# Two MLPs over 512-token groups with the weights stationary in every matmul

## The chip, the cores and the metric

The kernel runs on one core of a Trainium2 chip. The metric is the device time of one execution in microseconds; less is better. Its engines are named here as the profile names them: PE (TensorE matmuls) with PEld (its weight loads), DVE (VectorE), ACT (ScalarE), POOL (GpSimd) and SP (SyncE, which issues the transfers).

## What is computed

A linear attention with a complex decay over 4 batches x 8 heads x 768 steps of width 48, whose output is 3072 tokens of 384 values; then an MLP with a squared ReLU (384 to 2048 to 384); then a gated MLP (384 to 1536 twice, back to 384) behind an RMS normalisation.

```python
def _moe_ref(x, w_in, w_out):
    h = x @ w_in
    r = np.maximum(h, 0.0)
    g = r * r
    return (g @ w_out).astype(np.float32)

def _moe2_ref(x, w_gate, w_val, w_out, rms_g):
    rms = np.sqrt(np.mean(x * x, axis=-1, keepdims=True) + 1e-06)
    xn = x / rms * rms_g
    g = xn @ w_gate
    silu = g * (1.0 / (1.0 + np.exp(-g)))
    val = xn @ w_val
    return (silu * val @ w_out).astype(np.float32)
...
    attn_out = _attn_ref(**attn_kwargs)
    x = attn_out.transpose(0, 2, 1, 3).reshape(B * S, H * D)
    x = _moe_ref(x=x, **moe_kwargs)
    return _moe2_ref(x=x, **moe2_kwargs)
```

## The kernel before

**Units.** The 3072 tokens are 24 units of 128. A unit `u` is one batch and one stretch of 128 steps; attention makes units in order, two (a pair) sharing the long element-wise chain on DVE and ACT (`norm`, seven `step`s, `tot`, `plevel`, `inv`). The per-unit part runs on PE with DVE and ACT between: `dtr` (tile dps), `score` (sps, then st on DVE), `yy` (yps), `state` (ups). From yps the output goes to `xt` (ACT), six small transfers on SP put its rows in place (`fix`), and `split_x` cuts it into a high and a low half, `xs[:, 0]` on ACT and `xs[:, 1]` on DVE. That DVE subtraction is the last step of a unit; from then on the first MLP can use it.

**Three passes.** Every product of the MLPs is three fp32r matmuls, high x high, high x low and low x high (`PASS`), so nine matmuls of 128 contraction rows make one 384-long product.

**First MLP.** It takes a group of two units (256 tokens, `GROUPS`) at a time. For each of 16 slices `f` of the hidden width, `mlp_h` runs nine matmuls with a weight block stationary and 256 tokens moving, into tile h of PSUM (3 buffers). ACT makes r, the square's high half (gs) and the full square back into h; DVE subtracts to get the low half (L821). `mlp_x` follows: six matmuls (two units x three passes) with the activations gs stationary and 384 columns of the second weight moving, so that x has tokens on the partitions. `store_x` writes x to DRAM (`xnd`, one token a row).

**Second MLP.** It takes three units (384 tokens, `G2`). `load_x` reads rows of `xnd`; `rms` squares and sums each row on ACT (`accum_out`) and scales it on DVE; `turn` transposes it on PE (three transposes for each of three column blocks, tile t) and ACT and DVE split it into ys. For each of 12 slices `mlp_g` and `mlp_v` run nine matmuls of 384 tokens with weights stationary, ACT takes the SiLU (tile t), DVE multiplies (uu), ACT and DVE split (us), and `mlp_o` runs nine matmuls with us stationary and 384 weight columns moving. `store` writes the rows of the output.

**What sets the order.** The program is in straight line. `Plan` holds jobs, each a generator of steps with an engine, a cost, buffers taken and given back, and needs; it simulates the engines and writes the instructions in the order that it finds, so each engine's queue is fixed when the program is built. A group's first `mlp_h` needs the xs of all its units (`need` in the loop over groups). Matmuls of the MLPs have a lower urgency than those of attention (`MLP_PE`). While attention runs, PE has both kinds of work; after it, MLP work alone. The weights arrive as words that are converted on ACT and DVE (`convert`); for the second MLP their tiles take the place of the first MLP's as the last group lets go of them.

Of the kernel before, what the change touches and what calls it, by code (L numbers as in the profile page):

```python
# [18 lines left out]
CH = 128  # L19
# [18 lines left out]
GROUPS = [[2 * i, 2 * i + 1] for i in range(12)]  # L38
# [11 lines left out]
def act(n):  # L50
    return 0.1 + 0.00083 * n
# [509 lines left out]
def general_path(tc, q, k, v, a_re, a_im, w, ident, gcol, out):  # L561
# [3 lines left out]
    with ExitStack() as ctx:  # L565
# [63 lines left out]
        with ExitStack() as c2:  # L629
# [33 lines left out]
            with tc.For_i(0, NT // 128, 1) as it:  # L663
# [22 lines left out]
                acc = ps.tile([128, DM], F32, tag="gacc", name="g_acc2")  # L686
                for f in range(F2):
# [5 lines left out]
                    nc.tensor.matmul(acc, lhsT=g, rhs=words(T_OUT2 + f // 2, f % 2), start=(f == 0), stop=(f == F2 - 1))  # L693
                o = sb.tile([128, DM], F32, tag="go", name="g_o")
                nc.vector.tensor_copy(o, acc)
                nc.sync.dma_start(out[bass.ds(it * 128, 128), :], o)
# [3 lines left out]
def kernel_body(ctx: ExitStack, tc, q, k, v, vt, a_re, a_im, w, rms_g, out):  # L700
# [8 lines left out]
    xnd = dram.tile([NT, DM], F32, name="xnd")  # L709
# [4 lines left out]
    psh = p1.enter_context(tc.tile_pool(name="psh", bufs=3, space=PSUM))  # L714
# [9 lines left out]
        sY=2, pe=4, xt=1, xs=2, h=3, xg=1, r=2, gs=3, x1=2, cr=2, cr2=4, xr=2, gv=3, ys=2, og=1, t=2, uu=2, us=3, ot=3,  # L724
# [60 lines left out]
    def fix(u, g, i):
        xt, sl = xt_t[g], slice(i * CH, (i + 1) * CH)
# [5 lines left out]
    def split_x(u, g, i):  # L792
        sl = slice(i * CH, (i + 1) * CH)
        xs = xs_t[g]
        yield from split(
            xs[:, 0, :, sl], xs[:, 1, :, sl], xt_t[g][:, 0:KT, sl], DM, rel=["xt"] if i else [], done=("xs", u)
        )

    def mlp_h(g, f):
        n = len(GROUPS[g]) * CH  # L800
        yield Op("pe", 1.06, acq=["h"], rel=["xs"] if f == F1 - 1 else [], done=("h", g, f), p=MLP_PE)
# [34 lines left out]

    def store_x(g, i, u):
        if i == 0:
            yield Op("dve", dve(DM), acq=["x1"], done=("xc", g, i))
            x = sb.tile([128, DM], F32, tag="x1", name="x1", bufs=2)  # L840
            nc.vector.tensor_copy(x, x_ps[g][i])
        else:
            yield Op("act", act(DM), acq=["x1"], done=("xc", g, i))
            x = sb.tile([128, DM], F32, tag="x1", name="x1", bufs=2)
            nc.scalar.copy(out=x, in_=x_ps[g][i])
# [282 lines left out]
```

## Time and profile before

| what | value |
|---|---|
| median of 3 runs | 1147.71 us (1145.86 to 1148.03) |
| span of the profiled execution | 1147.8 us |
| PE busy | 1084.5 us, 94% |
| PEld busy | 1039.6 us, 91% |
| DVE busy | 720.2 us, 63% |
| ACT busy | 628.3 us, 55% |
| POOL busy | 100.6 us, 9% |

The profiled execution's span lies within the three runs, 0.1 us from their median. The shares are averages over stages that differ: attention and the first MLP run together up to some 628 us, the end of the first MLP and the second MLP after it. So the rows below are read stage by stage: a table of busy time by stretches, the starts of matmuls in a timeline (the distance of two starts is what a group of matmuls takes; the durations in it overlap), and groups of instructions by shape.

### The profile page before, as it was taken

The page shows a single profiled execution, that of the slowest core. Times are in us where ns is not written, and L with a number is a line of the kernel's source. Part 1 is how long each engine was busy: PE and PEld are TensorE (multiplying, and loading weights), DVE is VectorE, ACT ScalarE, POOL GpSimd, SP SyncE. Part 2 cuts the span into 40 slices and gives each one's busy share as a digit, 9 for nine tenths or more (in the row PEclk, how much of TensorE's full clock was granted, in tenths as well). Part 3 has the DMA queues.
Part 4 walks back from the last instruction along what each step waited for, and adds up shares of the span by engine and source line. Part 5 has one row for each costly group of instructions (what it writes and reads, how often), then busy time and mean ns, then how long its engine had stood idle before and what let it go on. Part 6 is the DMA issues. An engine that isn't in the chain of part 4 may idle for free.

```text
span 1147.8 us, 20154 instructions
## 1 busy us (share of the span) xinstructions
PE 1084.5 (94%) x7876; PEld 1039.6 (91%) x7876; DVE 720.2 (63%) x1468; ACT 628.3 (55%) x1387; POOL 100.6 (9%) x90
## 2 busy tenths in 40 slices
PE   1679889999999999999999999999999999999997
PEld 0468679999999999999999988999999999999997
DVE  5999999998989988998622579632323232222221
ACT  3878866668577766665655899432323232222221
POOL 0011123022121221220000000000000000000000
PEclk9799999999999999999999999999999999999999
DMA  8733141423514423331001780010101000000000
GB/s 276 302 87 103 33 127 47 121 55 107 143 40 121 113 68 102 87 88 38 23 11 40 253 331 2 9 33 10 33 11 32 11 32 11 12 11 11 13 9 24
DMA packets 79063, 85.41 MB, mean 74 GB/s; under 512 B 47728, under 2 KB 74608, under 8 KB 78960
## 3 DMA queue, kind: packets, MB, share of 16 engines
q1 hardware_dynamic: 78824, 83.85, 23.8%
q8 instruction: 64, 1.05, 0.4%
q14 instruction: 39, 0.32, 0.1%
q10 hardware_dynamic: 136, 0.20, 0.1%
HBM read 64.23 MB, written 18.61 MB: 72 GB/s over the span
## 4 chain that ended last, share of the span: by engine, by line
PE 83%; DVE 6%; ACT 5%; DMA 3%; issue 1%; SPq 1%; DVEq 0%; ACTq 0%
PE h L807 17%; PE x L832 17%; PE v L992 12%; PE o L1028 12%; PE g L992 12%; PE sps L467 3%; PE dps L454 3%; DMA ws<-in_w 3%; PE yps L484 2%; PE ups L502 2%; PE yps L488 2%; ACT ws L535 1%; DVE ws L537 1%; DVE cr L541 1%; ACT cr L533 1%
## 5 line engine op out<-in xcount | busy, mean ns | idle before, releaser
L807 PE MATMUL h<-xs,w 128*128 128x256 f32 x1728 | 242.2, 285 | 3.0 <-ACT w L761 1.8
L832 PE MATMUL x<-w,gs 128*128 128x384 f32 x1152 | 241.3, 344 | 2.3 <-ACT gs L817 1.3
L807 PEld LDWEIGHTS h<-xs,w 128*128 128x128 f32 x1728 | 224.8, 189 | 7.0 <-ACT w L761 2.4
L832 PEld LDWEIGHTS x<-w,gs 128*128 128x128 f32 x1152 | 194.1, 190 | 6.8 <-DVE gs L821 2.2
L1014 DVE TENSOR_TENSOR uu<-t,v 128x384 f32<-128x384 f32 x96 | 53.1, 554 | 195.8 <-PE v L992 194.5
L1028 PE MATMUL o<-w,us 128*128 128x384 f32 x864 | 166.9, 336 | 2.9 <-ACT us L729 2.5
L992 PE MATMUL g<-ys,w 128*128 128x384 f32 x864 | 167.0, 337 | 1.3 <-DVE w L731 0.5
L992 PE MATMUL v<-ys,w 128*128 128x384 f32 x864 | 167.4, 338 | 0.0
L1028 PEld LDWEIGHTS o<-w,us 128*128 128x128 f32 x864 | 151.0, 188 | 5.1 <-ACT us L729 3.1
L992 PEld LDWEIGHTS g<-ys,w 128*128 128x128 f32 x864 | 151.7, 188 | 2.7 <-DVE w L731 1.4
L992 PEld LDWEIGHTS v<-ys,w 128*128 128x128 f32 x864 | 150.3, 188 | 0.1
L814 ACT ACTIVATE r<-h 128x256 f32<-128x256 f32 x192 | 72.9, 380 | 122.9 <-PE h L807 122.4
L1005 ACT ACTIVATE t<-g 128x384 f32<-128x384 f32 x96 | 47.3, 493 | 159.9 <-PE g L992 159.8
L729 ACT CAST us<-uu 128x384 fp32r<-128x384 f32 x96 | 49.2, 513 | 131.2 <-DVE uu L1014 131.2
L821 DVE TENSOR_TENSOR gs<-h,gs 128x256 fp32r<-128x256 f32 x192 | 80.4, 419 | 58.8 <-ACT h L819 57.9
L731 DVE TENSOR_TENSOR us<-uu,us 128x384 fp32r<-128x384 f32 x96 | 53.6, 558 | 50.2 <-ACT us L729 50.2
L817 ACT ACTIVATE gs<-r 128x256 fp32r<-128x256 f32 x192 | 80.3, 418 | 8.7 <-PE x L832 2.7
L512 POOL TENSOR_TENSOR Y<-W,pe 48x384 f32<-48x384 f32 x40 | 52.1, 1302 | 320.3 <-DVE W L508 174.6
L819 ACT ACTIVATE h<-r 128x256 f32<-128x256 f32 x192 | 71.2, 371 | 0.0
L467 PE MATMUL sps<-dq,dk 112*128 112x128 f32 x384 | 52.6, 282 | 4.3 <-ACT dq L456 1.8
L467 PEld LDWEIGHTS sps<-dq,dk 112*128 112x128 f32 x384 | 49.3, 197 | 6.2 <-ACT dq L456 2.7
L300 DVE TENSOR_TENSOR XY<-A 128x384 f32<-128x384 f32 x84 | 49.0, 583 | 2.2
(123 smaller groups left out, 1338.7 us busy)
## 6 DMA issues: line engine op xcount, KB each, us to landing
ws<-in_w SPq DMA_DIRECT2D x34, 768.0 KB
kb<-KP SPq DMA_DIRECT2D x20, 448.0 KB
kt<-kb SPq DMA_DIRECT2D x20, 448.0 KB
raw<-in_a_re SPq DMA_DIRECT2D x24, 192.0 KB
raw<-in_a_im SPq DMA_DIRECT2D x24, 192.0 KB
kin<-in_k SPq DMA_DIRECT2D x24, 192.0 KB
qin<-in_q SPq DMA_DIRECT2D x24, 192.0 KB
V<-in_vt SPq DMA_DIRECT2D x24, 192.0 KB
```

The source lines that it names most:

```text
L467: nc.tensor.matmul(P[:, i], lhsT=K[:, h, :], rhs=Q[:, h, :], start=True, stop=True)
L512: nc.gpsimd.tensor_tensor(out=Y[dst:dst + D], in0=W[src:src + D], in1=im[src:src + D].to_broadcast([D, H, D]), op=ALU.mult)
L731: nc.vector.tensor_tensor(out=lo, in0=src, in1=hi.bitcast(F32), op=ALU.subtract)
L807: nc.tensor.matmul(hp, lhsT=part(f, 0, a)[:, kk * 128:(kk + 1) * 128], rhs=xs[:, bb, kk, :], start=(i == 0), stop=(i == 8),)
L814: nc.scalar.activation(out=r, in_=hp, func=AF.Relu)
L817: nc.scalar.activation(out=gs[:, 0], in_=r, func=AF.Square)
L819: nc.scalar.activation(out=hp, in_=r, func=AF.Square)
L821: nc.vector.tensor_tensor(out=gs[:, 1], in0=hp, in1=gs[:, 0].bitcast(F32), op=ALU.subtract)
L832: nc.tensor.matmul(x_ps[g][i], lhsT=gs[:, a, i * CH:(i + 1) * CH], rhs=part(f, 1, bb), start=(f == 0 and n == 0), stop=(f == F1 - 1 and n ...
L992: nc.tensor.matmul(P, lhsT=part(T_GATE + f, half, a)[:, kk * 128:(kk + 1) * 128], rhs=ys[:, bb, kk, :], start=(i == 0), stop=(i == 8),)
L1014: nc.vector.tensor_tensor(out=uu, in0=t_t.pop((g, f)), in1=P, op=ALU.mult)
L1028: nc.tensor.matmul(o_ps[g][i], lhsT=us[:, a, i * CH:(i + 1) * CH], rhs=part(T_OUT2 + f // 2, f % 2, bb), start=(f == 0 and n == 0), stop=( ...
```

## The change

Both MLPs work on 512 tokens where they can, and in every matmul of theirs a 128x128 block of the weights is stationary while the tokens move.

- `GROUPS` of the first MLP: two groups of two units, then five of four units. `mlp_h` is the same with 256 or 512 columns. `mlp_x` calls `turned_out`: for each of three blocks of output columns, three matmuls with a block of the second weight stationary and gs moving. x so has its 384 columns on the partitions and tokens along the free axis, in three PSUM tiles; to make room, h has 2 buffers instead of 3, and gs 2 instead of 3. `xnd` is kept transposed.
- `G2` of the second MLP: six groups of four units. `load_x` reads a transposed block in one transfer, so `turn` and its transposes go. The sum over a token's 384 values now runs across partitions: ACT squares (128x1536), DVE adds the three blocks and splits the sum, PE multiplies it by a matrix of ones (`rsum`, two matmuls of 512 columns), and DVE and ACT form the inverse root for all 128 partitions at 512 columns. `mlp_o` uses `turned_out`; the output is stored transposed and turned back on the host.
- `cr2` (conversion of the second MLP's weights) has 3 buffers instead of 4; one more ACT instruction at the start makes the ones.

```diff
-GROUPS = [[2 * i, 2 * i + 1] for i in range(12)]
+GROUPS = [[0, 1], [2, 3]] + [list(range(u, u + 4)) for u in range(4, 24, 4)]
+OF = {u: (g, us.index(u)) for g, us in enumerate(GROUPS) for u in us}
+
+
+def mm(k, n):
+    return k * (0.006 + 0.0004375 * n)
...
-    psh = p1.enter_context(tc.tile_pool(name="psh", bufs=3, space=PSUM))
+    psh = p1.enter_context(tc.tile_pool(name="psh", bufs=2, space=PSUM))
...
-        yield Op("pe", 1.06, acq=["h"], rel=["xs"] if f == F1 - 1 else [], done=("h", g, f), p=MLP_PE)
+        yield Op("pe", mm(9, n), acq=["h"], rel=["xs"] if f == F1 - 1 else [], done=("h", g, f), p=MLP_PE)
...
+        gs = sb.tile([128, 2, n], F32R, tag="gs", name="gs", bufs=2)
...
-    def mlp_x(g, f):
-        nb = len(GROUPS[g])
-        yield Op("pe", 1.06, acq=[] if f else ["xg"], rel=["gs"], done=("x", g, f), p=MLP_PE)
-        if f == 0:
-            x_ps[g] = [psx.tile([128, DM], F32, tag=f"x{i}", name=f"x{i}") for i in range(nb)]
-        gs = g_t.pop((g, f))
-        for i in range(nb):
+    def turned_out(ps, w, src, first, last):
+        for e in range(KT):
             for n, (a, bb) in enumerate(PASS):
                 nc.tensor.matmul(
-                    x_ps[g][i], lhsT=gs[:, a, i * CH:(i + 1) * CH], rhs=part(f, 1, bb),
-                    start=(f == 0 and n == 0), stop=(f == F1 - 1 and n == 2),
+                    ps[e], lhsT=w(bb)[:, e * 128:(e + 1) * 128], rhs=src[:, a, :],
+                    start=(first and n == 0), stop=(last and n == 2),
                 )
 
...
+    def mlp_x(g, f):
+        n = len(GROUPS[g]) * CH
+        yield Op("pe", mm(9, n), acq=[] if f else ["xg"], rel=["gs"], done=("x", g, f), p=MLP_PE)
+        if f == 0:
+            x_ps[g] = [psx.tile([128, n], F32, tag=f"x{e}", name=f"x{e}") for e in range(KT)]
+        turned_out(x_ps[g], lambda bb: part(f, 1, bb), g_t.pop((g, f)), f == 0, f == F1 - 1)
...
-    for g in range(NP):
+    NG = len(GROUPS)
+    START = [sum(len(x) for x in GROUPS[:g]) * F1 // 2 for g in range(NG)]
+    for g, us in enumerate(GROUPS):
         for f in range(F1):
-            s = F1 * g + f + MLP
-            need = [("xs", 2 * g), ("xs", 2 * g + 1), ("w", f, 0)]
+            s = START[g] + f * len(us) // 2 + MLP
+            need = [("xs", u) for u in us] + [("w", f, 0)]
...
-    G2 = [[3 * i, 3 * i + 1, 3 * i + 2] for i in range(8)]
-    xr, ys_t, t_t, u_t, o_ps, v_ps = {}, {}, {}, {}, {}, {}
+    G2 = [[4 * i + j for j in range(4)] for i in range(6)]
+    N2 = 4 * CH
...
+        sb, x = P2["sb"], xr[g]
+        yield Op("act", act(KT * N2), acq=["ys", "red"])
+        ys = ys_t[g] = P2["late" if g % 2 else "sb"].tile([128, 2, KT, N2], F32R, tag="ys", name="ys", bufs=1)
+        sq = sb.tile([128, KT, N2], F32, tag="rs_q", name="rs_q", bufs=1)
+        nc.scalar.activation(out=sq, in_=x, func=AF.Square)
...
+        yield Op("dve", dve(N2))
+        nc.vector.tensor_tensor(out=s, in0=sq[:, 0], in1=sq[:, 1], op=ALU.add)
+        yield Op("dve", dve(N2))
+        nc.vector.tensor_tensor(out=s, in0=s, in1=sq[:, 2], op=ALU.add)
+        yield from split(hl[:, 0], hl[:, 1], s, N2)
+        yield Op("pe", mm(2, N2), acq=["gv"])
+        P = P2["psg"].tile([128, N2], F32, tag="gv", name="rsum")
+        for i in range(2):
+            nc.tensor.matmul(P, lhsT=ones, rhs=hl[:, i], start=(i == 0), stop=(i == 1))
...
-        for i in range(len(G2[g])):
-            nc.tensor.transpose(P[:, i * CH:(i + 1) * CH], xr[g, i][:, kk * 128:(kk + 1) * 128], ident)
```

The same planner lays out both programs, so the change also moves instructions that the diff doesn't name. Three places, in the words of the program's order (line, operation, out<-in, size of the output, count).

PE before, at the start of the third group (units 4 and 5; x_1674 is the second group's sum, x_2281 the third's):

```order
L807 MATMUL h<-xs,w 128x256 x9
L454 MATMUL dps<-ident,KP_90 112x128 x4
L832 MATMUL x_1674<-w,gs 128x384 x3
L832 MATMUL x_1675<-w,gs 128x384 x3
L807 MATMUL h<-xs,w 128x256 x18
L832 MATMUL x_2281<-w,gs 128x384 x3
L832 MATMUL x_2282<-w,gs 128x384 x3
L454 MATMUL dps<-ident,KP_90 112x128 x4
```

PE after, from the second group's last x (x_1772 to x_1774) to the third group's first h (units 4 to 7):

```order
L844 MATMUL x_1774<-gs,w 128x256 x3
L459 MATMUL dps<-ident,KP_91 112x128 x4
L472 MATMUL sps<-dq,dk 128x128 x8
L459 MATMUL dps<-ident,KP_92 112x128 x8
L489 MATMUL yps<-st,V_89 64x128 x2
...
L321 MATMUL tot<-ident,A_87 48x128 x4
...
L489 MATMUL yps<-st,V_90 64x128 x2
...
L370 MATMUL back<-ident,TP 128x112 x2
...
L824 MATMUL h<-xs,w 128x512 x9
```

Before, the third group's h stand right behind the second group's last x, with one half of a transposition between. After, 57 rows of attention alone (units 6 and 7) stand there, and no matmul of an MLP.

DVE after, the same stretch, from the second group's last gs to unit 7's xs (50 rows, of which the ends are shown):

```order
L838 TENSOR_TENSOR gs<-h,gs 128x256
L433 TENSOR_TENSOR KP_92<-A_88,kin 128x8x48 x2
L433 TENSOR_TENSOR QP<-A_88,qin 128x8x48 x2
L861 COPY x_2304<-x_1773 128x256
...
L382 TENSOR_TENSOR x<-A_87,back 128x768 x2
L382 TENSOR_TENSOR A_87<-A_87,back 128x768 x2
L384 TENSOR_TENSOR A_87<-A_87,x 128x768
L386 TENSOR_TENSOR A_87<-A_87,x 128x768
L433 TENSOR_TENSOR QP<-A_87,qin 128x8x48
L745 TENSOR_TENSOR xs<-xt,xs 128x3x128
```

DVE before, the rows that end at the same xs of unit 7:

```order
L821 TENSOR_TENSOR gs<-h,gs 128x256
L307 TENSOR_TENSOR A_87<-XY 128x96
L300 TENSOR_TENSOR XY<-A_87 128x384
...
L841 COPY x_2879<-x_2281 128x384
L428 TENSOR_TENSOR QP<-A_86,qin 128x8x48 x2
L731 TENSOR_TENSOR xs<-xt,xs 128x3x128
```

Before, gs rows of the MLP run through to the end of the stretch (the last one ten rows ahead of xs). After, none stands among the last 50, and the work on the next pair that surrounds xs is another part of its chain.

PE before, in the second MLP, where a block of the next three units is transposed:

```order
L992 MATMUL g<-ys,w 128x384 x9
L978 MATMUL t<-ident,xr 128x128 x3
L992 MATMUL v<-ys,w 128x384 x9
L1028 MATMUL o_9128<-w,us 128x384 x3
L1028 MATMUL o_9129<-w,us 128x384 x3
```

PE after, in the second MLP, where the next group's sums are made:

```order
L844 MATMUL o_7621<-us,w 128x512 x3
L989 MATMUL rsum<-rs_h,ones 128x512 x2
L1013 MATMUL g<-ys,w 128x512 x9
L1013 MATMUL v<-ys,w 128x512 x9
L844 MATMUL o_8090<-us,w 128x512 x3
```

The transposes stood between a g and its v, three times a group (24 places); the sums stand once a group (6 places).

## Rows read from the trace of the kernel before

**Rows 1.** Busy time by stretches: length, then PE, PEld, DVE, ACT, POOL, clock.

```profile
core 0: us, PE busy (x) PEld busy (x) DVE busy (x) ACT busy (x) POOL busy (x), PEclk, DMA share, GB/s
79.50:163.60 84.10, 74.57 (x536) 62.08 (x536) 78.55 (x134) 66.94 (x138) 19.34 (x16) 0.96 0.29 78
163.60:260.30 96.70, 95.99 (x876) 92.86 (x874) 90.34 (x202) 65.21 (x162) 21.02 (x16) 1.00 0.33 89
260.30:441.70 181.40, 181.40 (x1678) 175.19 (x1677) 164.80 (x350) 123.96 (x303) 39.04 (x32) 1.00 0.35 96
441.70:628.50 186.80, 186.80 (x1616) 181.49 (x1615) 124.59 (x272) 113.27 (x280) 19.30 (x16) 1.00 0.18 51
628.50:1140.90 512.40, 507.50 (x2984) 502.56 (x2982) 197.39 (x371) 209.30 (x420) 0.00 (x0) 1.00 0.14 47
```

**Rows 2.** Timeline of PE, first MLP without attention: start, duration, line, operation.

```profile
622.99 1.23 PE L807 MATMUL h<-xs,w 128*128 128x256 f32 x9
624.06 1.21 PE L832 MATMUL x<-w,gs 128*128 128x384 f32 x6
625.10 1.23 PE L807 MATMUL h<-xs,w 128*128 128x256 f32 x9
```

**Rows 3.** Timeline of PE, second MLP.

```profile
903.56 1.72 PE L1028 MATMUL o<-w,us 128*128 128x384 f32 x9
...
908.23 1.73 PE L1028 MATMUL o<-w,us 128*128 128x384 f32 x9
...
911.37 0.49 PE L978 MATMUL t<-ident,xr 128*128 128x128 f32 x3
911.62 1.82 PE L992 MATMUL v<-ys,w 128*128 128x384 f32 x9
913.28 1.74 PE L1028 MATMUL o<-w,us 128*128 128x384 f32 x9
```

**Rows 4.** Timeline of DVE: the last step of units 1, 3, 7 and 15.

```profile
78.99 0.55 DVE L731 TENSOR_TENSOR xs<-xt,xs 128x384 fp32r<-128x384 f32 x1
...
163.57 0.55 DVE L731 TENSOR_TENSOR xs<-xt,xs 128x384 fp32r<-128x384 f32 x1
...
259.80 0.55 DVE L731 TENSOR_TENSOR xs<-xt,xs 128x384 fp32r<-128x384 f32 x1
...
441.16 0.55 DVE L731 TENSOR_TENSOR xs<-xt,xs 128x384 fp32r<-128x384 f32 x1
```

**Rows 5.** Groups by line and shape: count, busy us, mean ns, idle before them.

```profile
L821 DVE TENSOR_TENSOR gs<-h,gs 128x256 fp32r<-128x256 f32 x192 | 80.4, 419 | 58.8 <-ACT h L819 57.9
L469 DVE TENSOR_TENSOR st<-sps,mask 128x512 f32<-128x512 f32 x48 | 32.8, 686 | 13.6 <-PE sps L467 13.4
L256 ACT ACTIVATE m<-raw 128x768 f32<-128x768 f32 x12 | 10.1, 839 | 1.3 <-DMA raw<-in_a_re 1.3
L258 DVE TENSOR_TENSOR m<-m,A 128x768 f32<-128x768 f32 x12 | 12.1, 1006 | 6.0 <-ACT A L256 6.0
```

**Rows 6.** Timeline of PE at the start of the second group.

```profile
154.24 1.09 PE L484 MATMUL yps<-st,V 128*64 128x128 f32 x16 [1.00 <-DVE st L469]
...
163.17 0.62 PE L807 MATMUL h<-xs,w 128*128 128x256 f32 x3 [0.54 <-ACT xs L729]
164.18 3.14 PE L807 MATMUL h<-xs,w 128*128 128x256 f32 x24 [0.39 <-DVE xs L731]
```

**Rows 7.** The stretches of Rows 1, instructions on tile h alone (same columns, without POOL).

```profile
441.70:628.50 186.80, 80.29 (x576) 75.13 (x576) 26.92 (x64) 47.71 (x128) 1.00 0.18 51
628.50:1140.90 512.40, 24.87 (x180) 23.67 (x180) 8.88 (x21) 15.66 (x42) 1.00 0.14 47
```

**Rows 8.** The same, instructions on tile x alone.

```profile
441.70:628.50 186.80, 79.87 (x386) 64.27 (x385) 14.04 (x16) 1.91 (x4) 1.00 0.18 51
628.50:1140.90 512.40, 27.94 (x138) 22.89 (x136) 1.11 (x2) 0.95 (x2) 1.00 0.14 47
```

**Rows 9.** Timeline at the end: the last output transfer is issued.

```profile
1140.67 1.21 ACTq L1043 DMA_DIRECT2D out<-ot  x1
```

More of the change, by code (lines that the diff above doesn't have):

```diff
@@ L685, in general_path @@
                 xt = turned(x1, gcol)
-                acc = ps.tile([128, DM], F32, tag="gacc", name="g_acc2")
+                acc = [ps.tile([128, 128], F32, tag=f"gacc{e}", name=f"g_acc{e}") for e in range(KT)]
                 for f in range(F2):
@@ L692, in general_path @@
                     nc.vector.tensor_tensor(out=g, in0=g, in1=vp, op=ALU.mult)
[L693 to L696, printed above, removed]
+                    wo = words(T_OUT2 + f // 2, f % 2)
+                    for e in range(KT):
+                        nc.tensor.matmul(
+                            acc[e], lhsT=wo[:, e * 128:(e + 1) * 128], rhs=g, start=(f == 0), stop=(f == F2 - 1)
+                        )
+                o = sb.tile([128, KT, 128], F32, tag="go", name="g_o")
+                for e in range(KT):
+                    nc.vector.tensor_copy(
+                        o[:, e].rearrange("e (j p) -> e p j", j=8), acc[e].rearrange("e (p j) -> e p j", j=8)
+                    )
+                    nc.sync.dma_start(out[e * 128:(e + 1) * 128, bass.ds(it * 128, 128)], o[:, e])
 @with_exitstack
@@ L971, in turn @@
[L971 to L986 removed]
+        yield Op("sp", 0.65, acq=["xr"], mb=0.79, done=("xr", g))
@@ L1017, in mlp_v @@
[L1017 removed]
+        us = P2["sb"].tile([128, 2, N2], F32R, tag="us", name="us", bufs=3)
+        yield from split(us[:, 0], us[:, 1], uu, N2, rel=["uu"], done=("us", g, f))
         u_t[g, f] = us
     def mlp_o(g, f):
[L1021 to L1022 removed]
+        yield Op("pe", mm(9, N2), acq=[] if f else ["og"], rel=["us"], done=("o", g, f), p=MLP_PE)
@@ L1023, in mlp_o @@
         if f == 0:
-            o_ps[g] = [P2["pso"].tile([128, DM], F32, tag=f"o{i}", name=f"o{i}") for i in range(nb)]
-        us = u_t.pop((g, f))
-        for i in range(nb):
-            for n, (a, bb) in enumerate(PASS):
-                nc.tensor.matmul(
-                    o_ps[g][i], lhsT=us[:, a, i * CH:(i + 1) * CH], rhs=part(T_OUT2 + f // 2, f % 2, bb),
-                    start=(f == 0 and n == 0), stop=(f == F2 - 1 and n == 2),
-                )
-    def store(g, i):
-        b, c = att.bc(G2[g][i])
-        yield Op("dve" if i == 1 else "act", dve(DM), acq=["ot"], done=("oc", g, i))
-        t = P2["sb"].tile([128, DM], F32, tag="ot", name="ot", bufs=3)
-        if i == 1:
-            nc.vector.tensor_copy(t, o_ps[g][i])
-        else:
-            nc.scalar.copy(out=t, in_=o_ps[g][i])
-        end = (g, i) == (len(G2) - 1, 2)
-        yield Op("act" if end else "sp", 0.65, mb=0.2, rel=["ot"])
-        (nc.scalar if end else nc.sync).dma_start(
-            out[b * S_LEN + c * CH:b * S_LEN + (c + 1) * CH, :].rearrange("(p j) e -> j p e", j=8), t
-        )
+            o_ps[g] = [P2["pso"].tile([128, N2], F32, tag=f"o{e}", name=f"o{e}") for e in range(KT)]
@@ new lines, in mlp_o, with store @@
+        turned_out(o_ps[g], lambda bb: part(T_OUT2 + f // 2, f % 2, bb), u_t.pop((g, f)), f == 0, f == F2 - 1)
+    def store(g, e):
+        yield Op("dve" if e == 1 else "act", dve(N2), acq=["ot"], done=("oc", g, e))
+        t = P2["late"].tile([128, N2], F32, tag="ot", name="ot", bufs=3)
+        if e == 1:
+            nc.vector.tensor_copy(t, o_ps[g][e])
+        else:
+            nc.scalar.copy(out=t, in_=o_ps[g][e])
+        end = (g, e) == (len(G2) - 1, 2)
+        yield Op("act" if end else "sp", 0.65, mb=0.27, rel=["ot"])
+        dst = out[e * 128:(e + 1) * 128].rearrange("e (b c t) -> e b c t", b=B, c=NC)[:, :, g, :]
+        (nc.scalar if end else nc.sync).dma_start(dst, t.rearrange("e (b t) -> e b t", b=B))
@@ L1058, in kernel_body @@
         for f in range(F2):
             s = t0 + f
-            ys = [("ys", g, kk) for kk in range(KT)]
             before = [("v", g, f - 1)] if f else [("v", g - 1, F2 - 1)] if g else []
-            plan.job(s, mlp_g(g, f), ys + [("w", T_GATE + f)] + before)
+            plan.job(s, mlp_g(g, f), [("ys", g), ("w", T_GATE + f)] + before)
             plan.job(s + 0.1, mlp_v(g, f), [("g", g, f)])
```

191 lines of the change are left out of this document (91 added, 100 removed).

## The prediction, made before the changed kernel ran

> **What bounds the kernel now.** I read the table by stretches first. From 163.6 us to the last output PE is busy nearly all the time: 181.40 of 181.40 us and 186.80 of 186.80 us in the third and fourth stretch, 507.50 of 512.40 in the last [rows 1]. So the time is PE's, and a microsecond of matmuls saved is a microsecond saved, as long as PE has work. The same table shows the second thing to see: up to 441.7 us DVE is busy too, 78.55 of 84.10, 90.34 of 96.70 and 164.80 of 181.40 us, which leaves it idle for 6.6%, 6.6% and 9.2%. There attention's element-wise chain is almost as long as PE's work. From 441.7 us it falls behind PE, and after 628.5 us DVE and ACT are busy for less than half. So before 441.7 us a matmul saved is worth something only if DVE delivers units soon enough; after it, all of it.
>
> **What a matmul costs.** In the first MLP nine matmuls of 256 columns start 1.07 us before the next group and six of 384 columns 1.04 us: 119 and 173 ns each [rows 2]. In the second, 27 of 384 columns take 908.23 - 903.56 = 4.67 us, 173 ns again, stationary weights or stationary activations alike [rows 3]. [...] A line through 119 and 173 gives 0.42 ns a column and 11 ns a matmul, so 227 ns at 512 columns. No row has 512 columns in this type, so the bounds are 216 ns (the fixed part gone) and 231 ns (173 x 512/384, nothing gained by width); I take 227, since two shapes lie on the line.
>
> **First MLP, PE alone.** Before: 192 slices (12 groups x 16) at 1.07 + 1.04 us, 405.1 us. After: 32 slices with 18 matmuls of 256 columns, 2 x 1.07 us each, 68.5 us, and 80 slices with 18 of 512 columns, 80 x 18 x 0.227 = 326.9 us. Gain 9.7 us.
>
> **Second MLP, PE alone.** Before: 96 slices at 4.67 us, 448.3 us. After: 72 x 27 x 0.227 = 441.3 us. Gain 7.0 us. Where three transposes stand, o to o takes 913.28 - 908.23 = 5.05 us and not 4.67 [rows 3]: 0.38 us at 24 places, 9.1 us, go; 12 matmuls by ones, 2.7 us, come. Gain 6.4 us.
>
> Together 23 us, which by itself gives 1147.8 - 23.1 = 1125 us. The new RMS puts 11 DVE instructions of 512 columns a group (0.69 us each by the 512-column row) and one of 1536 (2 x 1.01 us) on DVE, and two of 1536 (2 x 0.84 us each) with two of 512 on ACT [rows 5]: some 10 and 5 us a group, 60 and 30 us in all, under an idle of 315 and 303 us in the last stretch [rows 1]. The cover is those idle engines; where the 2 us instruction stands ahead of a product's split, o can wait for it, at most 6 x 2 us. I take nothing for that, as the saved waits of the transposes' chain stand against it. The transfers get longer rows and fewer issues and lie off the path; the last output transfer alone stands at the end, 6.9 us before it from 1140.9 us [rows 1, 9], and with shorter pieces I add 0.5 us.
>
> **Where the gain goes: groups of four must wait for four units.** The order shows it. Before, the third group's first h follow the second group's last x at once. After, 57 rows of attention alone stand between, and two more such stretches come at the fourth and fifth group (23 and 30 rows); from the sixth group on, h of the next stands among x of the last. At the first, PE's rows are 190 matmuls at 0.078 us (51.4 us for 654 in the fourth stretch, below), 15 us, while DVE has 58 instructions to unit 7's xs, at its mean of 168.9 us for 336 in the first two stretches [rows 1] 29 us, less for the short ones among them, say 25; also from a unit's yps to the h that it releases 164.18 - 155.33 = 8.9 us pass, in transfers and the split [rows 6]. So PE stands idle some 10, 5 and 3 us there. Before has one such wait, at the second group, 9.5 us of idle in the first stretch of the table [rows 1].
>
> Until the fifth group's first h (units 12 to 15) I therefore count DVE. It is released by the xs of unit 15, at 441.16 us before [rows 4]. Between unit 1's xs (78.99 us) and this one DVE has 680 rows before and 656 after. The difference: 107 gs of 256 columns become 32 of 256 and 32 of 512, -75 x 0.419 + 32 x 0.686 = -9.5 us (the 512 price by st, which reads PSUM at 512 columns; if it is 2 x 0.419, +4.9 us) [rows 5]; the copies of x -1 us; and 7.7 us of attention rows more, for the planner runs further ahead with the next pair. In sum -2.8 us: the same work. DVE's busy time to this point is 333.7 us [rows 1], so 331 us after. At 6.6% idle, as where it set the pace, that takes 354 us; at the 7.9% of the three stretches together, 359 us. From 79.5 us on that is 434 to 439 us, and with 0.6 us to the first h [rows 6] I take 437 us.
>
> What is left from there, first **before, from 441.7 us**: 706.1 us. In the fourth stretch 576 x 0.119 + 386 x 0.173 = 135.4 us are MLP [rows 7, 8], the other 51.4 us attention; in the last stretch 180 x 0.119 + 138 x 0.173 = 45.3 us belong to the first MLP, 448.3 + 9.1 to the second, and 9.7 us are waits and the like; 6.9 us end it. **After, from 437 us**: three groups of the first MLP, 3 x 16 x 18 x 0.227 = 196.1 us; attention 51.4 us less 5 us (64 of its matmuls more are done by then, of 654 in that stretch); 441.3 + 2.7 us of the second MLP; waits 9.7 us as before; 7.4 us at the end; and 2 us at the last group, whose h must wait for unit 23 behind three slices of x (3 x 2.04 us against 8.9 us). Sum 705.6 us. So 437 + 706 = **1143 us**, 0.4% less than the span of 1147.8 us, which stands 0.1 us from the median. The change gives PE 23 us, and 18 of these are lost while PE waits for units.
>
> [...]
>
> **Rivals.** First, **DVE gets ahead** (faster). With fewer MLP matmuls in PE's queue, dps, sps and yps come back sooner, and DVE's idle share falls to 4%: 331/0.96 = 345 us, the fifth group at 425 us, the end at 1131 us. For it: in the stretches without MLP PE does attention at once. Against: in the first stretch, where PE was not full, DVE still was idle for 6.6%.
>
> Second, **PE and DVE wait for each other** (slower). With 2 buffers of h and gs, the square of slice f+2 waits for x of slice f at the head of ACT's queue, and behind it stands attention's work for DVE. Its place is the third and fourth group, where PE's own sum (2 x 65.4 us and attention) is as long as DVE's. If DVE is idle 10.5% there as everywhere to 441 us, 331/0.895 = 370 us, the fifth group starts at 450 us and the end is 1156 us. For it: the third stretch had 9.2% with 3 buffers [rows 1]. Against: PE then will stand idle at each group's start, which is when DVE catches up. It turns slower than before from 441.7 us, that is at an idle share of 8.5%.
>
> Third, **width gains nothing**: 231 ns. From the fifth group on 864 + 1944 = 2808 matmuls run at 512 columns, and 4 ns more are 11 us: 1154 us. Fourth, **the fixed 11 ns vanish**: 216 ns, 31 us less, 1112 us. [...] Against both: two shapes give the same line.
>
> **How the numbers follow.** Forecast (1137 to 1149 us) 0.46; DVE ahead 0.20; waiting for each other 0.24; no gain by width 0.06; fixed part gone 0.04. The range 1128 to 1157 us leaves about 0.2 outside. A measurement of this kernel can tell some 0.2% (2.3 us) from no change. Below 1145.4 us lie the two faster rivals and nearly two thirds of the forecast, 0.53; within 0.2% a third of it and a little of the others, 0.20; above, 0.27.
>
> **What would show it.** 512-column groups of nine should start 2.04 us apart, and an o in the second MLP 6.13 us after the o before it. Unit 15's xs at 434 to 439 us shows the DVE count right; well below 430 the first rival, beyond 443 the second. PE should be idle some 10 us before the third group's first h and little after the fifth's. I am wrong if the stall before the third group is absent, or if PE waits in the second MLP for the sums by ones.

## The result, and the profile after

The changed kernel takes 1157.57 us (1155.16 to 1158.0, four runs) against 1147.87 us in the same job: ratio 1.0075, interval 1.0054 to 1.0095. It is **slower by 9.7 us**; the forecast was 1143 us, 4 to 5 us faster. The profiled execution has a span of 1155.9 us and a time of its own of 1157.69 us, so 1.8 us lie outside the span. That also holds for the kernel before: its runs of 1148.02 and 1147.71 us have spans of 1146.3 and 1145.9 us. The profiled execution of the kernel before, with its span of 1147.8 us, thus took some 1149.5 us and not the median, and the forecast of 1143 us, added up from spans, has these 1.7 us missing.

Busy time of the changed kernel by stretches, cut at the first h of each group from the second on, then at the last x (length, then busy time of PE, PEld, DVE, ACT and POOL, clock):

```profile
core 0: us, PE busy (x) PEld busy (x) DVE busy (x) ACT busy (x) POOL busy (x), PEclk, DMA share, GB/s
79.50:160.40 80.90, 73.49 (x597) 61.94 (x596) 74.75 (x130) 65.21 (x134) 21.04 (x18) 0.96 0.35 92
160.40:232.30 71.90, 62.50 (x639) 58.48 (x639) 64.48 (x147) 42.39 (x106) 11.47 (x10) 0.97 0.31 82
232.30:345.90 113.60, 107.51 (x732) 88.33 (x732) 97.98 (x190) 65.66 (x124) 22.94 (x20) 0.94 0.35 93
345.90:446.40 100.50, 98.49 (x732) 80.62 (x732) 89.47 (x190) 60.80 (x117) 18.39 (x18) 1.00 0.36 93
446.40:533.70 87.30, 87.26 (x619) 72.19 (x619) 77.18 (x155) 52.93 (x99) 17.47 (x14) 1.00 0.26 69
533.70:626.30 92.60, 91.31 (x552) 76.09 (x549) 35.24 (x62) 44.25 (x79) 0.00 (x0) 1.00 0.06 20
626.30:706.10 79.80, 77.90 (x339) 62.85 (x339) 65.40 (x85) 71.53 (x107) 0.00 (x0) 1.00 0.58 198
706.10:1147.20 441.10, 441.08 (x1910) 358.05 (x1908) 150.82 (x216) 128.71 (x189) 0.00 (x0) 1.00 0.07 20
```

Against [rows 1] two things are new. In the second to fourth row PE is idle for 9.40, 6.09 and 2.01 us, where before it was idle for 0.71 us between 163.6 and 628.5; and the clock is 0.97 and 0.94 where it was 1.00. DVE is idle for 15.6 of 113.6 us in the third row, in which PE is busy for 107.5. Of PE's idle time 8.0, 4.0 and 1.5 us lie in the stretches of attention alone ahead of the third, fourth and fifth group:

```profile
209.20:232.30 23.10, 15.11 (x189) 12.50 (x188) 21.31 (x53) 10.44 (x24) 3.88 (x4) 0.92 0.53 136
328.20:345.90 17.70, 13.73 (x124) 11.55 (x122) 15.42 (x26) 6.97 (x13) 4.80 (x4) 0.81 0.55 153
435.90:446.40 10.50, 8.98 (x112) 7.34 (x112) 6.58 (x23) 6.58 (x13) 3.55 (x4) 1.00 0.74 198
```

The fifth group starts at 446.4 us; the forecast was 437.

PE around the start of the third group (start, duration, operation, wait before it), and the same place as stretches, before and while the clock is low; the last stretch lies ahead of the fourth group:

```profile
226.80 0.45 PE L370 MATMUL back<-ident,TP 112*128 112x112 f32 x2 [2.87 <-DVE TP L352]
230.05 1.91 PE L507 MATMUL ups<-V,kt 128*64 128x48 f32 x32 [2.80 <-DMA kt<-kb]
232.30 4.68 PE L824 MATMUL h<-xs,w 128*128 128x512 f32 x9 [0.34 <-ACT xs L743]
...
242.90 2.36 PE L824 MATMUL h<-xs,w 128*128 128x512 f32 x9 [2.02 <-DVE gs L838]
```

```profile
210.00:228.60 18.60, 12.92 (x154) 10.69 (x154) 16.84 (x47) 9.39 (x22) 3.88 (x4) 1.00 0.58 147
228.60:238.80 10.20, 8.30 (x48) 6.46 (x49) 9.06 (x13) 5.11 (x8) 4.02 (x3) 0.50 0.14 40
...
337.80:344.70 6.90, 6.22 (x28) 5.49 (x27) 4.87 (x11) 1.17 (x2) 0.00 (x0) 0.51 0.59 147
```

PE waits for attention's small steps (2.87 us for TP, 2.80 us for a transfer). It is idle for 5.7 of 18.6 us up to 228.6 us; then its granted clock falls to 0.50 for 10.2 us, and the first nine h take 4.68 us where nine later ones take 2.36. Before the fourth group the clock is 0.51 for 6.9 us, from 337.8 us on; ahead of the fifth, with PE idle for 1.5 of 10.5 us, it is 1.00. What makes the clock fall is not shown.

PE in the second MLP, in two token groups (the distance of two starts is what nine matmuls take):

```profile
806.86 2.21 PE L1013 MATMUL g<-ys,w 128*128 128x512 f32 x9
808.91 2.20 PE L1013 MATMUL v<-ys,w 128*128 128x512 f32 x9
810.95 2.27 PE L844 MATMUL o<-us,w 128*128 128x512 f32 x9
813.05 2.21 PE L1013 MATMUL g<-ys,w 128*128 128x512 f32 x9
...
901.18 2.26 PE L1013 MATMUL g<-ys,w 128*128 128x512 f32 x9
903.28 2.26 PE L1013 MATMUL v<-ys,w 128*128 128x512 f32 x9
905.38 2.26 PE L844 MATMUL o<-us,w 128*128 128x512 f32 x9
907.48 2.26 PE L1013 MATMUL g<-ys,w 128*128 128x512 f32 x9
```

In the second token group (from 806 us) g and v take 2.05 and 2.04 us, 227 ns a matmul, and o takes 2.10 us, 233 ns; in the third (from 901 us) all three take 2.10 us. PE never waits there (none of g, v and o has idle time before it in the whole trace), so the sums by ones hold nothing up. Two prices for one shape: that was the first thing to explain.

### The profile page after: what moved, and what is told of

The parts are those of the page before. It is cut to its first block, busy times and chain, and to the rows that moved or that the text cites. A ratio compares the mean times of both kernels' runs of the same rounds, so it can differ in the third digit from the quotient of the medians.

```text
span 1155.9 us, 16403 instructions
## 1 busy us (share of the span) xinstructions
PE 1078.1 (93%) x6304; PEld 884.5 (77%) x6304; DVE 720.5 (62%) x1317; ACT 582.4 (50%) x1040; POOL 93.2 (8%) x90
## 4 chain that ended last, share of the span: by engine, by line
PE 80%; DVE 12%; ACT 4%; issue 2%; DMA 1%; SPq 1%; DVEq 0%; ACTq 0%
PE h L824 15%; PE x L844 14%; PE o L844 13%; PE g L1013 13%; PE v L1013 13%; PE sps L472 3%; PE dps L459 3%; PE yps L489 2%; PE ups L507 1%; PE yps L493 1%; DVE ws L542 1%; DVE gs L838 1%; DVE XY L305 1%; PE lo L772 1%; DMA ws<-in_w 1%
## 5 line engine op out<-in xcount | busy, mean ns | idle before, releaser
L824 PE MATMUL h<-xs,w 128*128 128x512 f32 (+1 forms) x1008 | 226.8, 371 | 8.6 <-DVE gs L838 5.1
L844 PE MATMUL x<-gs,w 128*128 128x512 f32 (+1 forms) x1008 | 221.1, 365 | 0.7 <-DVE gs L838 0.7
L844 PEld LDWEIGHTS x<-gs,w 128*128 128x128 f32 x1008 | 168.8, 189 | 29.1 <-DVE gs L838 1.3
L844 PE MATMUL o<-us,w 128*128 128x512 f32 x648 | 162.0, 395 | 0.0
L1013 PE MATMUL g<-ys,w 128*128 128x512 f32 x648 | 161.1, 393 | 0.0
L1013 PE MATMUL v<-ys,w 128*128 128x512 f32 x648 | 160.8, 392 | 0.0
L844 PEld LDWEIGHTS o<-us,w 128*128 128x128 f32 x648 | 121.6, 188 | 28.7
L834 ACT ACTIVATE gs<-r 128x512 fp32r<-128x512 f32 (+1 forms) x112 | 64.0, 571 | 78.6 <-PE x L844 67.3
L838 DVE TENSOR_TENSOR gs<-h,gs 128x512 fp32r<-128x512 f32 (+1 forms) x112 | 68.3, 610 | 48.7 <-ACT h L836 48.4
L831 ACT ACTIVATE r<-h 128x512 f32<-128x512 f32 (+1 forms) x112 | 59.9, 535 | 57.6 <-PE h L824 56.5
```

Of the source, the lines that this page charges most:

```text
L824: nc.tensor.matmul(hp, lhsT=part(f, 0, a)[:, kk * 128:(kk + 1) * 128], rhs=xs[:, bb, kk, :], start=(i == 0), stop=(i == 8),)
L838: nc.vector.tensor_tensor(out=gs[:, 1], in0=hp, in1=gs[:, 0].bitcast(F32), op=ALU.subtract)
L844: nc.tensor.matmul(ps[e], lhsT=w(bb)[:, e * 128:(e + 1) * 128], rhs=src[:, a, :], start=(first and n == 0), stop=(last and n == 2),)
L1013: nc.tensor.matmul(P, lhsT=part(T_GATE + f, half, a)[:, kk * 128:(kk + 1) * 128], rhs=ys[:, bb, kk, :], start=(i == 0), stop=(i == 8),)
```

## Experiments on the price of a matmul

Where the tiles lie gives a pattern. By the program's allocation, sixteen weight tiles of the second MLP begin at 2816 to 94976 bytes of a partition and the last two at 152544 and 158688; ys begins at 180192 for the token groups 1, 3, 5 and at 101120 for 2, 4, 6; us lies at 217056 and above. In the changed kernel's trace g and v mostly take 226 or 227 ns with ys at 101120 (means 227.8 and 226.8) and 231 to 235 with ys at 180192 (mean 233.3); in the one slice of twelve whose g and v read the tile at 158688, it is the other way round (means 233.1 and 233.5, and 228.6 and 226.7). o takes 231 to 235 (mean 233.4), but mostly 226 or 227 with the weight tile at 152544 (mean 229.1). The end of the third token group, where g, v and the first o read these tiles, shows it: they take 2.06, 2.04 and 2.05 us in a group that otherwise takes 2.10.

```profile
913.78 2.23 PE L1013 MATMUL g<-ys,w 128*128 128x512 f32 x9
915.84 2.20 PE L1013 MATMUL v<-ys,w 128*128 128x512 f32 x9
917.88 2.21 PE L844 MATMUL o<-us,w 128*128 128x512 f32 x9
919.93 2.23 PE L1013 MATMUL g<-ys,w 128*128 128x512 f32 x9
```

Low addresses (2816 to 101120 here) are multiples of 64 bytes and high ones (152544 and up) are 32 off, so there are two readings: the address modulo 64, or the part of SBUF, low or high.

**pad32** and **before_pad32** shift the second MLP's tiles by 32 bytes, in the changed kernel and in the one before.

```diff
+        pad = main.enter_context(tc.tile_pool(name="pad", bufs=1, side="right", reuse_waits="tile"))
+        pad = pad.tile([128, 8], F32, tag="pad", name="pad", bufs=1)
+        nc.gpsimd.memset(pad, 0.0)
         P2["sb"] = main.enter_context(tc.tile_pool(name="p2", ...))
```

> The changed kernel with an unused tile of 32 bytes a partition ahead of the second MLP's tiles on the right side of SBUF, so that ys and us begin at a multiple of 64 bytes, as most weight tiles do. Theory A, the addresses: in the trace of the changed kernel matmuls start 227 ns apart where the weight tile and the streamed tile have the same address modulo 64, and 231 to 235 where they differ (ys of the groups 0, 2, 4, and every us but the last slices'). Then nearly all of the second MLP goes to 227 ns, o to o from 6.23 to 6.13 us, 72 slices give 7 to 8 us, and the time is 1150 us. Theory W, the width: 231 ns is what 512 columns cost beside this work; o to o stays at 6.23 us and the time at 1157 us.

> The kernel before with the same 32 bytes ahead of its second MLP's tiles. Theory A: its ys and us differ modulo 64 from the weights too, so its 384-column matmuls (171 to 178 ns, mean 174) go to 172 to 173 ns; o to o from 4.69 to 4.65 us, 3 to 4 us in 96 slices, 1144 us. Theory W: nothing moves, 1147.9 us.

pad32: 1157.37 us, nothing gained, and the two prices stand at the same places as before the shift. before_pad32: 1151.65 us, ratio 1.0027 (1.0017 to 1.0037), 3.6 us above the 1148.06 us of the kernel before in the same job, so with a shift of 32 bytes the 384-column kernel was a little slower. The address modulo 64 isn't the reason for the two prices.

**low** and **before_low** move ys and us, after the first token groups, and the last two weight tiles to the low part. The lines that matter, of low:

```diff
-        ys = ys_t[g] = P2["late" if g % 2 else "sb"].tile([128, 2, KT, N2], ..., bufs=1)
+        ys = ys_t[g] = P2["late" if g else "sb"].tile([128, 2, KT, N2], ..., bufs=2 if g else 1)
...
-        us = P2["sb"].tile([128, 2, N2], F32R, tag="us", name="us", bufs=3)
+        us = P2["late" if g else "sb"].tile([128, 2, N2], F32R, tag="us", name="us", bufs=3)
...
-            plan.job(T2 - F1 - 4 + m - F1, load(n, m, lambda: P2["w"], ["open2"]))
+            plan.job(T2 - F1 - 4 + m - F1, load(n, m, lambda: P2["late"], ["open3"]))
```

> The changed kernel with ys and us from the second token group on, and the last two weight tiles, moved from the high part of SBUF (152544 bytes a partition and up) to the low part (101120 to 156416), where the other 16 weight tiles lie. In the traces of the changed kernel and of its padded twin the 227 ns pitch goes with a weight tile and a streamed tile that lie in the same part, and 231 to 235 with two that lie in different parts, whatever the address is modulo 64. Theory A2, the parts of SBUF: groups two to six go to 227 ns throughout, o to o 6.13 us, the second MLP 5 to 6 us shorter, 1152 us. Theory W, the width: o to o stays 6.2 to 6.3 us, 1157 us.

> The kernel before with its ys and us from the third token group on, and its last two weight tiles, in the low part of SBUF. Theory A2: its matmuls of 384 columns, now 173.7 (o), 174.2 (g) and 176.9 ns (v) in the slices, go to 172 to 173 ns; 72 slices x 27 x 2 ns = 4 us, 1144 us. If the part of SBUF matters only to 512 columns, or it goes with the address within the 64 bytes (its padded twin was 3.6 us slower), 1148 us or more.

low: 1150.85 us, ratio to the kernel before 1.0020 (1.0010 to 1.0030), 6.7 us less than the changed kernel. Its PE in the second MLP:

```profile
902.23 2.20 PE L844 MATMUL o<-us,w 128*128 128x512 f32 x9
904.27 2.20 PE L1013 MATMUL g<-ys,w 128*128 128x512 f32 x9
906.31 2.20 PE L1013 MATMUL v<-ys,w 128*128 128x512 f32 x9
908.35 2.20 PE L844 MATMUL o<-us,w 128*128 128x512 f32 x9
```

Every nine take 2.04 us, o to o 6.12 us. From the second token group on twelve slices take 73.93 to 74.04 us (12 x 6.12 and 0.46 for the two matmuls by ones are 73.9), where the changed kernel had 74.83 and 75.86 in turn. Theory A2 expected that; what in SBUF makes the difference is open. before_low: 1147.21 us, ratio 0.9992 (0.9981 to 1.0003): at 384 columns there is next to nothing to win (0.6 us of 1147.85), and the 4 us expected were wrong.

## Experiments on the groups

One row tells most: the stretch from 160 to 480 us, in which attention and the first MLP run together. The kernel before, then the changed one:

```profile
160.00:480.00 320.00, 318.08 (x2933) 306.55 (x2932) 292.03 (x621) 216.17 (x529) 67.66 (x55) 1.00 0.34 94
```

```profile
160.00:480.00 320.00, 302.46 (x2346) 255.61 (x2345) 282.49 (x575) 191.28 (x389) 58.96 (x54) 0.97 0.34 88
```

PE is idle for 17.5 us and not 1.9, and has the low clock in two stretches of 10.2 and 6.9 us, in which it is busy for 8.30 and 6.22 us (above): taken as half speed, that work loses 7.3 us, half of 14.52 (an estimate). Together with the 15.6 us of idle time that are new, this makes 22.9 us.

**pairs**: the first MLP in twelve groups of two, the second MLP as changed; copies of x have a tile of their own. **before_2buf**: the kernel before with only the two buffers of h and gs. The first edit below is that of pairs, the second that of before_2buf.

```diff
-GROUPS = [[0, 1], [2, 3]] + [list(range(u, u + 4)) for u in range(4, 24, 4)]
+GROUPS = [[2 * i, 2 * i + 1] for i in range(12)]
```

```diff
-psh = p1.enter_context(tc.tile_pool(name="psh", bufs=3, space=PSUM))
+psh = p1.enter_context(tc.tile_pool(name="psh", bufs=2, space=PSUM))
...
-        gs = sb.tile([128, 2, n], F32R, tag="gs", name="gs", bufs=3)
+        gs = sb.tile([128, 2, n], F32R, tag="gs", name="gs", bufs=2)
```

> The changed kernel with its first MLP in twelve groups of two units again (256 tokens; h and x both at 256 columns, weights stationary in both), the second MLP at 512 as changed; the copies of x get a tile of their own. Theory S, groups of four starve PE at their start and its clock falls there: no idle before a group after the second, granted clock 1.00 from 165 us on. By the two profiles the second MLP is 464 us before and 452 after, x at 256 columns costs 192 x (1.07 - 1.04) = 6 us more than before: 1147.8 - 12 + 6 = 1142 us. Theory B, two buffers of h and gs make PE and DVE wait for each other: DVE stays idle for 10% or more up to unit 15's xs, which comes at 450 us or later, and the time is 1150 us or more.

> The kernel before with two buffers of h and of gs in place of three, and nothing else. Theory B: DVE's idle share up to unit 15's xs rises from 7.9% to 10.5%, that xs comes 10 us later, at 451 us, and the time is 1157 us. Theory S: three buffers are not what kept PE busy; the time stays within 2 us of 1147.9 us.

before_2buf: 1150.63 us, ratio 1.0022 (1.0013 to 1.0032): two buffers cost 2.6 us, not 10, and unit 15's xs ends at 437.9 us, not later than before (441.7). The wait that theory B names is there all the same: ACT's square (gs) waits until x has let go of the buffer. Between 232 and 446 us, in this order in the kernel before, before_2buf, the changed kernel and sixpairs_low (the fastest, below):

```profile
ACT gs L817 <- PE x L832: 2.0, 1, 2.0
ACT gs L817 <- PE x L832: 22.7, 32, 2.0
ACT gs L834 <- PE x L844: 27.1, 17, 2.8
ACT gs L834 <- PE x L844: 24.6, 31, 2.0
```

It is nearly as long in the fastest kernel as in the changed one, so it isn't what sets them apart.

pairs: 1156.71 us, ratio 1.0071 (1.0050 to 1.0092). Half of theory S holds: the clock is 1.00 from 240 us on and unit 15's xs ends at 437.9 us. But the total is 15 us above its 1142. PE's waits from 400 to 700 us (total, times, longest) tell why:

```profile
PE h L824 <- DVE gs L838: 9.3, 8, 2.2
```

Here theory B is right, late: once there is little attention to fill PE, h of a group of 256 tokens with two buffers waits for the low half of the square (gs on DVE). Pairs are good early, and not late.

**threes**, **late_fours**: three pairs then six groups of three, and eight pairs then two fours. Both give the copies of x one buffer of their own.

```diff
+GROUPS = [[0, 1], [2, 3], [4, 5]] + [list(range(u, u + 3)) for u in range(6, 24, 3)]
...
+GROUPS = [[2 * i, 2 * i + 1] for i in range(8)] + [list(range(u, u + 4)) for u in range(16, 24, 4)]
```

> The changed kernel with its first MLP in three groups of two units and then six of three (384 columns for h and x). Matmuls of the first MLP: 48 slices x 18 x 0.119 + 96 x 18 x 0.173 = 402 us, 7 more than in the changed kernel. Theory S, starving at the start of a group of four: a group of three waits for fewer units, PE's idle time and the low clock between 160 and 450 us fall to less than half, unit 15's xs comes at 440 us, and the time is 1152 us. Theory B, two buffers: idle time of DVE stays at 11% there and the time is 1160 us or more.

> The changed kernel with its first MLP in eight groups of two units and only the last eight units in two groups of four. Theory S: up to unit 15's xs as with pairs alone (438 us), then the two groups of four save 32 x (4.28 - 4.09) = 6 us of matmuls and half of the 10 us that PE waited between 400 and 700 us in the kernel of pairs: 1156.7 - 11 = 1146 us. Theory B: the waits stay, 1151 us or more.

threes: 1148.44 us, ratio 0.9999 (0.9989 to 1.0009), better than theory S asked, though it has 7 us more matmuls than the changed kernel; PE is idle for 7.0 of the 320 us. late_fours: 1158.96 us, ratio 1.0091 (1.0072 to 1.0109), a miss of 13 us: PE is idle for 13.0 of the 320 us, 6.2 us of it in waits of h for gs and 2.4 us in waits of x for its own copies in the single buffer, so that kernel doesn't tell what a late group of four costs by itself.

**warm** puts matmuls of no use into PE's order to hold the clock up.

```diff
+        while not all(("xs", u) in plan.t for u in GROUPS[g]):
+            yield Op("pe", 0.65, need=[("w", 0, 0)], p=500.0)
+            for i in range(2):
+                nc.tensor.matmul(x_ps[g][0][:, 0:DM], lhsT=ones, rhs=part(0, 0, 0), start=True, stop=True)
```

> The changed kernel with matmuls that compute nothing of use (84 of 384 columns, 173 ns each, into the bank of x before x starts) set into PE's order where the planner sees PE idle before the third and the fourth group. Theory C, the clock: PE's granted clock stays 1.00 between 225 and 240 and between 337 and 345 us, where it was 0.5 for 17 us, the first h of these groups take 2.0 instead of 4.7 and 4.2 us, attention's matmuls there run at full speed, and the time falls by 6 to 9 us, to 1150 us. Theory D, it is the DVE chain that sets when the groups start and the clock only stretched what was idle: the starts of the third to fifth group move by less than 3 us and the time stays at 1155 us or above.

1162.02 us, ratio 1.0116 (1.0097 to 1.0135). The clock rose to 0.99 over the 320 us, and the time grew all the same, so theory C's gain did not come. But it isn't a clean test: the matmuls took PE's time in front of attention's steps, the planner laid the units out anew (unit 7's xs starts at 247.1 in place of 233.5 us), and the third group's first h came at 246.2 in place of 232.3 us. What the low clock alone costs stays open; 7.3 us is worked out, not shown.

**own_x**, the changed kernel with a tile of its own for the copies of x, which go out in halves of 256 columns:

```diff
-        x = sb.tile([128, n], F32, tag="r", name="x1", bufs=2)
...
+            x = sb.tile([128, 256], F32, tag="x1", name="x1", bufs=2)
```

> The changed kernel with one edit: the copies of x get a tile of their own (two buffers of 256 columns, each group's copy in two halves) in place of the two buffers of r, which the relu of the next group's h also needs. Groups and the second MLP as changed. Theory S, groups of four starve PE at their start whatever the copies do: unit 15's xs stays at 446 us, the time at 1157 us. Theory R, the shared buffers: the next group's relu waits until a copy of x has gone out by DMA, so part of the late start of the groups is this; unit 15's xs comes some 4 to 5 us earlier and the time is 1152 to 1153 us.

```profile
160.00:480.00 320.00, 303.47 (x2348) 257.52 (x2347) 286.12 (x583) 191.66 (x391) 58.52 (x54) 0.97 0.34 92
```

1158.66 us, ratio 1.0097 (1.0073 to 1.0121). Unit 15's xs does come 8 us earlier (438.3 in place of 446.6 us), as theory R has it, and the time doesn't fall: PE's idle time (16.5 us) and its clock are the same. So the fifth group's start, on which the prediction was built, isn't what sets the end. PE's lost time is: own_x starts the fifth group 7.2 us earlier (439.2 us), but from 79.5 us to there PE was busy for 335.9 us and not 342.0, so that 6.1 us of work were left for later.

## A kernel that is faster than both

**threes_low** joins threes and low, with two buffers for the copies of x. **sixpairs_low** has six pairs and four threes. **sixpairs_fours_low** has three fours behind the six pairs, with x copied in halves.

```diff
+GROUPS = [[2 * i, 2 * i + 1] for i in range(6)] + [list(range(u, u + 3)) for u in range(12, 24, 3)]
...
+GROUPS = [[2 * i, 2 * i + 1] for i in range(6)] + [list(range(u, u + 4)) for u in range(12, 24, 4)]
```

> The two steps together: the first MLP in three groups of two units and six of three, and ys, us and the last two weight tiles of the second MLP in the low part of SBUF from the second token group on; the copies of x have two buffers of their own in place of one. If the two gains are independent (threes 9.1 us, low 6.7 us), 1157.6 - 15.8 = 1142 us, faster than the kernel before by 6 us. If the shorter first MLP only hands its time to waits in the second, or the second x buffer changes the planner's order for the worse, 1148 us.

> As the kernel with threes and the low part, but six groups of two units and then only four of three. Theory S: if a group costs more the more units it waits for while DVE sets the pace (up to unit 15), pairs up to unit 11 start earlier and unit 15's xs comes before 438 us; they cost 24 us x (0.119 x 4 / 3 / 0.173 - ...) in matmuls as little as 1.5 us: 1140 us. Theory B: pairs with two buffers wait for gs, as in the kernel of pairs and the one with eight pairs; 1145 us or more.

> As the kernel with six pairs, then threes, and the low part, but with three groups of four after the six pairs, x copied out in halves of 256 columns with two buffers of their own. Theory S: a group of four costs waiting only while DVE's chain sets the pace; from unit 12 to 15 on that is nearly over. 48 x 18 x 0.227 against 64 x 18 x 0.173 us of matmuls save 3 us, one wait for four units costs some of it: 1133 to 1136 us. Theory F, fours wait wherever they stand: PE is idle 5 us or more before the first of them and the time is 1140 us or more.

threes_low: 1138.07 us, ratio 0.9910 (0.9894 to 0.9927). sixpairs_low: **1135.84 us**, ratio 0.9889 (0.9873 to 0.9906), 12 us under the kernel before. (In its expectation the price of the pairs is unfinished; 48 slices x 18 x 0.119 against 32 x 18 x 0.173 us are 3.2 us.) sixpairs_fours_low: 1150.55 us, ratio 1.0025 (1.0015 to 1.0036), theory F. sixpairs_low, then the one with fours:

```profile
160.00:400.00 240.00, 237.54 (x2371) 229.28 (x2370) 217.97 (x488) 161.64 (x399) 46.05 (x40) 1.00 0.35 93
400.00:480.00 80.00, 79.68 (x688) 76.47 (x688) 72.78 (x136) 49.62 (x111) 17.26 (x15) 1.00 0.32 89
```

```profile
160.00:400.00 240.00, 238.11 (x2354) 229.87 (x2353) 217.02 (x468) 158.83 (x399) 42.05 (x38) 1.00 0.33 91
400.00:480.00 80.00, 71.27 (x588) 60.83 (x587) 73.66 (x143) 46.73 (x94) 17.26 (x16) 0.94 0.30 82
```

Up to 400 us the two are alike. Where the first group of four stands, PE is idle for 8.7 us in place of 0.3 and the clock falls to 0.94. In these runs groups of four starve PE wherever attention still feeds them; groups of three there don't.

## Why the prediction was wrong, step by step

**The price of 512 columns: right with both tiles in one part of SBUF.** 227 ns, from the line through two shapes, is what the kernel low shows (2.04 us for nine), and the first MLP:

```profile
668.45 2.20 PE L844 MATMUL x<-gs,w 128*128 128x512 f32 x9
670.49 2.20 PE L824 MATMUL h<-xs,w 128*128 128x512 f32 x9
672.53 2.20 PE L844 MATMUL x<-gs,w 128*128 128x512 f32 x9
```

231 to 235 ns, the third rival's price, which I gave 0.06, is what some six in ten matmuls of the second MLP took, but not for that rival's reason: low has the same width at 227 ns. Twelve slices took 75.35 us on average in place of the 73.93 of low: 1.42 x 6 = 8.5 us. The step at fault is that one price was taken for all 512-column matmuls. The line also hid it: at 384 columns the place of the tiles is worth almost nothing (before_low: 1147.21 us for 1147.85), so the rows of before could not warn. The price in the first MLP was right (x to x above takes 4.08 us for 18 matmuls, 4.09 forecast), and so was the end of the transposes.

The fourth rival's price, 216 ns, did not come: the steady price here is 227 ns at best, the 2.04 us for nine of the kernel low and of the first MLP.

**PE's waits at the groups of four: the sizes held.** I had 10, 5 and 3 us; the stretches that end at these groups have 9.40, 6.09 and 2.01 us, of which 8.0, 4.0 and 1.5 us stand directly ahead of them. What I left out is the granted clock, 0.50 for 10.2 us and 0.51 for 6.9 us at the first two of these groups: 7.3 us more, worked out from the rows above and not shown by a run. I also misread the kernel before: the 9.5 us that I took for one wait at its second group are all the idle time of that stretch, in which PE's waits at that group's first h are 0.54 and 0.39 us [rows 6]. No sum uses that reading.

**The count of DVE: busy time right, idle share wrong.** DVE was busy for 326.7 us up to the fifth group (forecast 331). But I took its idle share from the kernel before, 6.6 to 7.9%, and it was 40.2 of 366.9 us, 11.0%. I had argued: "PE then will stand idle at each group's start, which is when DVE catches up". That step failed, and the fifth group came 9.4 us late. DVE is idle for 10.3% of the second row of the table, in which PE waits, and for 15.6 us in the third. In that third row (232.3 to 345.9 us) it waits for PE's sps and, longer in all, for ACT: 4.2 us for the square, 4.7 us for steps of its own chain. ACT itself waits for PE:

```profile
DVE gs L838 <- ACT h L836: 4.2, 4, 2.1
DVE st L474 <- PE sps L472: 4.1, 5, 1.5
...
ACT gs L834 <- PE x L844: 16.7, 11, 2.8
ACT r L831 <- PE h L824: 11.5, 11, 2.5
```

A reading that fits, but that no run tests by itself: once a late group has started, PE owes the group's matmuls and attention's at once, so DVE waits for PE, in part by way of ACT, and the time lost at the start doesn't come back.

**The second rival named nearly the right time (1156 us, 10.5% idle) for a reason that doesn't carry it.** Its sign was there too: unit 15's xs came at 446.6 us, beyond 443. ACT's wait for x is as it says, but two buffers cost 2.6 us in before_2buf, at 256 columns, and the same wait stands in sixpairs_low. Three buffers at 512 columns were not run. The size of the groups costs the most: from low to sixpairs_low the groups (and the second buffer for x) change, the time falls by 15.0 us, and sixpairs_low has 9.5 us more of first-MLP matmuls (96 x 18 x 0.119 + 64 x 18 x 0.173 = 405 us against 395). So some 24 us of waiting went, close to the 22.9 us read from the trace.

**The rest from the fifth group on:** 709.5 us for 705.6 forecast. 8.5 us are the price above, 1.3 us the end (8.7 us from PE's last matmul at 1147.2 us to the end of the span, for 7.4), 2.6 us what is left over in the first MLP with attention; against these PE waits for 3.2 us (700.8 us with 697.55 busy) where I had 11.7. own_x shows that the sum should not have been cut there at all: it starts the fifth group at 439.2 us, with more work left, and ends no earlier.

**In sum,** 9.4 us up to the fifth group, 3.9 us behind it and 1.8 us outside the span are the difference between forecast and result, 14.6 us, to half a microsecond. By cause, the gain of 23 us was 8.5 us smaller, and the loss at the groups 22.9 us (7.3 of them worked out) in place of 18.

## What to carry to other kernels

Here the line through two shapes gave a matmul a fixed part of 11 ns, of 227 at 512 columns, so fewer and wider matmuls save some of it; but a larger group waits for more of what feeds it (PE was idle for 9.40, 6.09 and 2.01 us in the stretches up to three groups of four). Where the feeder sets the pace, price the wait at the group's start, a clock that falls there (0.50 and 0.51 in this trace), and the feeder's own waits afterwards. Group sizes may change along the program: small while the feeder is the bound, larger when it no longer is (here pairs, then threes). Look at the starts of matmuls tile by tile: here the same shape had two prices, 227 and 231 to 235 ns, that followed where its tiles lie.

## What the runs showed of the hardware

All of this was measured in this case's runs. Low and high are names for the addresses that these programs use, by their allocation; where a border lies and what makes the difference is not shown.

- In the second MLP of the changed kernel a 512-column fp32r matmul with a weight load mostly took 226 or 227 ns with its weight tile and its moving tile both low (2816 to 113408 bytes of a partition; means 227.8 for g and 226.8 for v) or both high (152544 and up; means 228.6 for g, 226.7 for v, 229.1 for o), and 231 to 235 ns with one in each (means 233.1 to 233.5). In the kernel low, with both tiles at 2816 to 150272 bytes, nine took 2.04 us.
- A shift by 32 bytes left the two prices where they were at 512 columns (pad32, 1157.37 us for 1157.57) and went with 3.6 us more in the kernel of 384 columns (before_pad32, 1151.65 us for 1148.06).
- In the changed kernel PE's granted clock went to 0.50 for 10.2 us (228.6 to 238.8 us) behind a stretch in which PE had been idle for 5.7 of 18.6 us, with no single wait above 2.87 us, and to 0.51 for 6.9 us (337.8 to 344.7 us). It stayed at 1.00 in the kernel before from 150 to 165 us, where PE was idle for 4.4 of 15.0 us, so these runs give no rule for it.
